# Second batch's fourth key block issued between W1's two transfers, its sums and key turns behind other work, in a Linformer attention and expert kernel on one core

## Chip, cores and metric

One core of a Trainium2 chip. The time is device microseconds of one execution; the figure for the kernel before is the median of three runs, 407.22 us (406.07 to 408.49).

## The reference, cut to what matters

Eight batches of eight heads of attention with 32 memory rows, then a mixture of experts in which each token goes to one expert.

```python
a = phi - np.max(phi, axis=2, keepdims=True); a = np.exp(a)
a = a / (np.sum(a, axis=2, keepdims=True) + 1e-09)
k_m = np.einsum('bhsm,bhsd->bhmd', a, k)
v_m = np.einsum('bhsm,bhsd->bhmd', a, v)
scores = scale * np.matmul(q, k_m.transpose(0, 1, 3, 2))
attn = softmax(scores)
x = attn @ v_m                      # [8 batches x 576 tokens, 512]
logits = normalised(x) @ normalised(expert_emb).T / tau
e = argmax(logits)                  # one expert a token
out = gate * (relu(x @ w1[e]) @ w2[e])
```

## The kernel before

The program is unrolled over batches. Each batch is treated as one group of tokens with one expert e, chosen from the batch's scores; tokens of another expert are counted and redone in a branch at the end. Because x is attn times v_m, the kernel multiplies v_m by W1 first (`project`, L655, two parts of 512 hidden columns, tiles `pg`, results `gh` and `gl`) and then attn by that product (`first`, L670, tiles `ph`), then by W2 (`second`, L692, tiles `py`). All engines run their instructions in the order in which the program writes them down. Eight banks of PSUM are handed out by rotation: `pt` takes t0, t1, ... over `tags` banks, `mm` takes m0 to m3; a tile waits until the bank's last reader is done.

The change lies in the opening, L985 to L1066, and in `batch(0)`, L821:

- Batch 0's scores are made, its first 128 tokens alone are weighed (`weigh`, `divide`, `turn`), and `choose` (L203) reads the expert from them. SP then loads that expert's W1 in two transfers of 1 MB (`load_w1`, L438), one for each part of `project`.
- Before that, `load_kv(1)` (L414, called at L1015) has put batch 1's keys and values into SP's queue: two pieces `kl` and four blocks `kx` of 512 KB, all ahead of W1.
- `fill` (L60) is a vector transpose of the scores of tokens 128 to 575 out of PSUM (tile `tr`), for both groups of heads, at L1045, behind the choice.
- `owner` (L220) is two small vector instructions on the counts; it stands ahead of the second `divide`.
- `slots(1, ...)` (L509) sums batch 1's keys and values over all blocks on TensorE into `acc0t` and `acc0m`. `scale(1)` (L534, two ScalarE instructions) and `again` (L556, one GpSimd copy) follow, all ahead of `project`.
- Between the two parts of `project(0)` the program has `part` (L637: two ScalarE casts and two GpSimd differences for `aT`), `keys(1)` (L543: two transposes `tk`, one ScalarE copy `kT`), `values(1)` (L560: two transposes `tv`, four copies `vT`; it reads both halves that `again` completes) and `attend(1, 2)` (L108: products `po` of two token tiles, their transposes `tt`, and the choice's `lg`, `m`, `oh` on VectorE). `norm(0)` (L175, one fused VectorE instruction that reads the bank m2, which the second part of `project` takes) stands ahead of the first part.
- `warm` issues matmuls whose result nobody reads.

Of the kernel before, what the change touches and what calls it, by code (L numbers as in the profile page):

```python
# [19 lines left out]
P = 128  # L20
B, H, S, D, M = 8, 8, 576, 64, 32
N, DM, E, FF = B * S, H * D, 8, 1024
NG = 2
# [23 lines left out]
class Tokens:  # L47
# [115 lines left out]
            out=self.oh[:, i], in0=self.lg[:, i], in1=self.m[:, i].unsqueeze(2).broadcast_to((P, len(ti), E)), op=ALU.is_equal  # L163
        )

    def turned(self, *ti):

        k, nc, b = self.k, self.nc, self.b
        t = self.pt([P, len(ti), NG * P], f"tt{b}_{ti[0]}")
        for n, i in enumerate(ti):  # L170
            for g in range(NG):
                nc.tensor.transpose(t[:, n, P * g : P * g + P], k.aw[:, g, T0[i] : T0[i] + P], k.ident)
        nc.scalar.copy(k.ea[:, ti[0] : ti[-1] + 1], t)
# [102 lines left out]
class Kernel:  # L276
# [137 lines left out]
    def load_kv(self, b):  # L414
        if b < B:
            for g in range(NG):
                to, x = self.kl[64 * g : 64 * g + 64], self.kvt[b, :, 4 * g : 4 * g + 4]
                (self.nc.sync if b else self.nc.scalar).dma_start(to, x)
            for k in range(4):
                self.nc.sync.dma_start(self.kx[k], self.kv[b, :, k])  # L420

    def load_q(self, b, halves=(0, 1)):
        if not b:
# [14 lines left out]
    def load_w1(self, e, halves=False):  # L438

        for k in range(2 if halves else 4):  # L440
            c, f = (slice(NC), slice(512 * k, 512 * k + 512)) if halves else (slice(k, k + 1), slice(FF))
            self.nc.sync.dma_start(self.w1s[:, c, f], self.w1[bass.ds(e, 1), :, c, f].rearrange("a p c f -> (a p) c f"))

# [377 lines left out]
    def batch(self, b, t, u):  # L821

        first, second = self.steps(b, t, u)
        self.halves = 0

        def must(f):
            while self.halves <= f:
                self.split_w()

        if b and u:  # L830
            self.keys(b + 1)
            self.values(b + 1)
        for k, _ in enumerate(self.project(b, self.vT[b % 2]) if u else ()):
            if not b:
                for g in range(NG):
                    self.part(g, slice(HS, S) if k else slice(P, HS), self.nc.scalar.copy)
                if k:
                    t.norm(1, 2)
                else:
                    self.keys(1)  # L840
                    self.values(1)
                    t.attend(1, 2)
        if b and u:

            self.scores(b + 1)
        for n, _ in enumerate(self.first(b)):
            for step in first[n]:
                step()
        for n, _ in enumerate(self.second(b, self.gate[:, b], self.rows(b), must)):
            for step in second[n]:  # L850
                step()
            if n == 8 and b == B - 1:
                left = self.others()
            if n == 24 and b == B - 1:
                self.tc.mark_branch_hint_location("others", left[1], engines=[ET.PE, ET.DVE, ET.SP, ET.Activation])
        return left if b == B - 1 else None
# [123 lines left out]
@with_exitstack  # L980
def moe_linformer(ctx, tc, phiT, qT, kv, kvt, emb, tau, w1, w2, out):
    k = Kernel(ctx, tc, phiT, qT, kv, kvt, emb, tau, w1, w2, out)
    ctx.enter_context(tc.manual_schedule(engines={ET.PE, ET.DVE, ET.Activation, ET.SP, ET.Pool}))


    k.eights()
    k.warm(11)
    k.load_phi(0)
    k.load_kv(0)
    k.load_q(0)  # L990
    k.load_router()
    k.consts()
    accs = [k.ps.tile([P, 2 * D], F32, tag=f"{n}3", name=f"acc0{n}", bufs=1) for n in "tm"]
    for vT in k.vT:
        k.nc.vector.memset(vT, 0.0)
    router = k.router()
    for g in range(NG):
        k.largest(0, g)
        k.softmax(0, (g,))
    for i in (0, 4, 8):  # L1000
        k.turn(0, i, min(i + 4, 9))
        if not i:
            next(router)
        if i < 8:
            k.warm(2 if i else 4)
    k.shares(0)
    next(router)
    k.load_phi(1)
    t = Tokens(k, 0, k.pt)
    for ks in ((0, 1), (4,), (2,), (3,)):  # L1010
        k.slots(0, accs, ks=ks, first=0 in ks, last=3 in ks)
        if ks[0] < 3:
            k.warm(2 if ks[0] == 2 else 1)
    k.scale(0)
    k.load_kv(1)  # L1015
    k.keys(0)
    k.again()
    first, others = slice(0, 4), slice(4, BL)
    ts = [k.mm([P, P], f"ts0_{g}", 1 + g) for g in range(NG)]
    k.score(0, ts, 0, P)  # L1020
    t.fill(range(NG), first, ts)
    next(router, None)
    k.values(0, copy=k.nc.scalar.copy)
    ts = [k.mm([P, S - P], f"tr0_{g}", g) for g in range(NG)]
    k.score(0, ts, P, S)
    k.squares(0, [k.pt([P, D + E], f"tl0_{g}") for g in range(NG)])
    list(t.weigh(range(NG), first))
    k.products(0)
    k.warm(5, 2)
    t.divide(range(NG), first)  # L1030
    t.turn(range(NG), first)
    k.largest(1, 0)
    k.softmax(1, (0,))
    t.attend(0, pt=lambda shape, name: k.mm(shape, name, 2), turned=False)
    e = t.choose((0,))
    t.turned(0)
    k.largest(1, 1)
    k.softmax(1, (1,))
    k.load_q(1, (0,))
    for i in (0, 4, 8):  # L1040
        k.turn(1, i, min(i + 4, 9))
        k.turns += not i
        if not i:
            k.warm(7, hot=t.spare)
    t.fill(range(NG), others, ts)  # L1045
    weights = [t.weigh((g,), others) for g in range(NG)]
    for g in range(NG):
        next(weights[g])
    for g in range(NG):
        next(weights[g])  # L1050
        list(weights[g])
    t.owner()
    k.shares(1, v=k.nc.gpsimd)
    for g in range(NG):
        k.part(g, slice(0, P), k.nc.scalar.copy)
    k.slots(1, accs)
    k.tags = 4
    k.scale(1)
    k.again(k.nc.gpsimd.tensor_copy)
    t.divide(range(NG), others, True)  # L1060
    t.turn(range(NG), others)
    t.norm(0)
    k.load_w2(e)
    k.load_q(1, (1,))
    k.load_phi(2)
    k.warm(3)  # L1066
    for b in range(B):
        u = Tokens(k, b + 1, k.pt) if b < B - 1 else None
        left = k.batch(b, t, u)
        t = u  # L1070
    k.rest(*left)
# [29 lines left out]
```

## Time and profile before

| what | value |
|---|---|
| median of three runs | 407.22 us |
| the profiled execution's own time | 406.74 us |
| its span, first to last instruction | 404.9 us |
| TensorE busy | 393.5 us, 97% of the span |
| VectorE, ScalarE, GpSimd busy | 65%, 39%, 42% |
| DMA, mean over the span | 225 GB/s |

The profile has a row for every instruction with its engine, line, tile and, where the engine stood idle before it, what released it. PE is TensorE's matmul row and PEld its weight loads; SPq is SP's queue, whose rows are the issue of a transfer and not its data.

### The profile page before, as it was taken

The numbers are of one execution on the slowest core, as the hardware profiler recorded it, in microseconds if no ns is written. First come the engines' busy times: TensorE is split into PE (matmuls) and PEld (weight loads), VectorE is DVE, ScalarE is ACT, GpSimd is POOL, SyncE is SP. The second block draws the span as 40 slices with busy tenths as digits, with TensorE's granted clock in tenths as the row PEclk, the third lists the DMA queues.
The fourth block names the chain that finished last, engine by engine and source line by source line (L and its number), as shares of the span: only waits on it lengthen the run. The fifth ranks groups of instructions, "written<-read, shape, count | busy, mean of one in ns | idle before, by whom it ended". The sixth has DMA issues, their size and how long they took to land. (4 is left out here: it accounts for less than half of the span.)

```text
span 404.9 us, 10350 instructions
## 1 busy us (share of the span) xinstructions
PE 393.5 (97%) x3933; PEld 318.5 (79%) x3933; DVE 262.3 (65%) x909; ACT 157.2 (39%) x430; POOL 171.2 (42%) x205
## 2 busy tenths in 40 slices
PE   7889999999999999999999999999999999999995
PEld 3458877798777978879787888879788897879784
DVE  4698795769664794758855795747936595745000
ACT  4366623165313633147311753137231561146110
POOL 1036563187133940369121961349303681329300
PEclk9999999999999999999999999999999999999999
DMA  8999927995679925995469926798359404790011
GB/s 265 345 363 357 375 61 183 342 358 212 149 255 386 349 46 132 346 384 234 74 215 389 387 82 160 251 388 338 56 137 361 178 2 81 249 396 6 14 53 56
DMA packets 69862, 91.24 MB, mean 225 GB/s; under 512 B 41800, under 2 KB 47688, under 8 KB 69808
## 3 DMA queue, kind: packets, MB, share of 16 engines
q1 hardware_dynamic: 66928, 82.00, 60.9%
q0 software_dynamic: 2688, 8.26, 5.8%
q8 instruction: 32, 0.52, 0.5%
q10 hardware_dynamic: 192, 0.28, 0.2%
q14 instruction: 22, 0.18, 0.1%
HBM read 71.19 MB, written 19.33 MB: 224 GB/s over the span
## 5 line engine op out<-in xcount | busy, mean ns | idle before, releaser
L681 PE MATMUL ph<-aT,gh 128*128 128x288 f32 x512 | 103.2, 297 | 0.0
L734 PE MATMUL py<-wh,hh 128*128 128x512 f32 x248 | 99.3, 400 | 0.0
L734 PE MATMUL py<-wh,hl 128*128 128x512 f32 x248 | 96.7, 390 | 0.0
L734 PE MATMUL py<-wl,hh 128*128 128x512 f32 x248 | 96.7, 390 | 0.0
L652 POOL TENSOR_TENSOR wl<-w2s,wh 128x512 fp32r<-128x512 f32 x64 | 85.1, 1330 | 5.0
L681 PEld LDWEIGHTS ph<-aT,gh 128*128 128x128 f32 x512 | 81.8, 188 | 1.7 <-DVE oh L162 0.8
L681 PE MATMUL ph<-aT,gl 128*128 128x288 f32 x256 | 75.4, 294 | 0.0
L687 DVE SCALAR_TENSOR_TENSOR hl<-ph,hh 128x288 fp32r<-128x288 f32 x128 | 55.8, 450 | 22.1 <-ACT hh L684 16.7
L739 ACT ACTIVATE ys<-py,gate 128x512 f32<-128x512 f32 (+1 forms) x39 | 25.1, 642 | 105.3 <-PE py L734 70.3
L684 ACT ACTIVATE hh<-ph 128x288 fp32r<-128x288 f32 x128 | 52.4, 417 | 31.9 <-PE ph L681 31.6
L868 POOL DMA_DIRECT2D out_dram<-ys x28 | 15.5, 553 | 106.1 <-ACT ys L739 69.4
L734 PEld LDWEIGHTS py<-wh,hh 128*128 128x128 f32 x248 | 46.5, 188 | 14.6 <-issue 4.9
L734 PEld LDWEIGHTS py<-wh,hl 128*128 128x128 f32 x248 | 46.6, 188 | 10.1
L734 PEld LDWEIGHTS py<-wl,hh 128*128 128x128 f32 x248 | 46.6, 188 | 9.0
L681 PEld LDWEIGHTS ph<-aT,gl 128*128 128x128 f32 x256 | 48.0, 188 | 0.0
L642 POOL TENSOR_TENSOR aT<-aw,aT 128x576 fp32r<-128x576 f32 (+3 forms) x20 | 23.7, 1204 | 48.4 <-DVE aT L641 42.8
L651 POOL CAST wh<-w2s 128x512 fp32r<-128x512 f32 x62 | 38.6, 622 | 1.0 <-DMA w2s<-w 0.9
L723 PE MATMUL py<-w2s,h 128*64 128x256 f32 x256 | 29.4, 382 | 0.0
L665 DVE TENSOR_TENSOR gl<-pg,gh 128x512 fp32r<-128x512 f32 x32 | 20.0, 684 | 8.7 <-ACT gh L664 8.7
L723 PEld LDWEIGHTS py<-w2s,h 128*64 128x64 f32 x256 | 17.7, 137 | 9.3 <-DVE hl L687 1.0
L472 ACT ACTIVATE ex<-ex,nm 128x576 f32<-128x576 f32 x16 | 12.3, 771 | 29.5 <-DVE nm L457 29.5
L664 ACT CAST gh<-pg 128x512 fp32r<-128x512 f32 x32 | 16.5, 599 | 10.5 <-PE pg L662 10.5
(180 smaller groups left out, 468.9 us busy)
## 6 DMA issues: line engine op xcount, KB each, us to landing
kx<-kv SPq DMA_DIRECT2D x32, 512.0 KB, 7.5
w2s<-w SPq DMA_DIRECT2D x32, 512.0 KB, 9.8
w1s<-w SPq DMA_DIRECT2D x28, 512.0 KB, 6.4
out_dram<-ys POOLq DMA_DIRECT2D x28, 256.0 KB, 6.1
qt<-qT SPq DMA_DIRECT2D x12, 576.0 KB, 8.8
ad<-aw SPq DMA_DIRECT2D x8, 576.0 KB, 12.5
td<-x SPq DMA_DIRECT2D x56, 72.0 KB, 2.1
ea<-td SPq DMA_DIRECT2D x7, 512.0 KB, 4.4
```

The costliest lines, as they stand in the source:

```text
L642: self.nc.gpsimd.tensor_tensor(out=al, in0=a, in1=ah.bitcast(F32), op=ALU.subtract)
L651: (copy or self.nc.scalar.copy)(h, x)
L652: self.nc.gpsimd.tensor_tensor(out=l, in0=x, in1=h.bitcast(F32), op=ALU.subtract)
L664: nc.scalar.copy(self.gh[:, g, f], ps[g])
L665: nc.vector.tensor_tensor(out=self.gl[:, g, f], in0=ps[g], in1=self.gh[:, g, f].bitcast(F32), op=ALU.subtract)
L681: nc.tensor.matmul(p, lhsT=w[:, g, fs], rhs=x[:, g, to], start=g == 0 and k == 0, stop=g == 1 and k == 2)
L684: nc.scalar.activation(self.hh[:, f, to], p, AF.Relu)
L687: nc.vector.scalar_tensor_tensor(out=self.hl[:, f, to], in0=p, scalar=0.0, in1=self.hh[:, f, to].bitcast(F32), op0=ALU.max, op1=ALU.subtract)
L723: nc.tensor.matmul(p[64 * j : 64 * j + 64], lhsT=self.h4[:, f], rhs=self.w2s[:, f, d * j : d * j + d], start=f == 0, stop=f == 7,)
L734: nc.tensor.matmul(p, lhsT=h[:, f, to], rhs=w[:, f], start=f == 0 and k == 0, stop=f == 7 and k == 2)
L739: nc.scalar.activation(y[:, :d], p, AF.Copy, scale=gate[:, i : i + 1])
L868: eng.dma_start(self.out[r : r + P], y)
```

## The change

Batch 1's fourth block `kx[3]` is issued between W1's two transfers. Its sum stands behind the first part of `project(0)`, and so do `scale(1)`, `again` and `norm(0)`. `keys(1)` and `values(1)` go behind `attend(1, 2)`, and the transposes `tt` of those two token tiles take the bank m0 instead of a t bank. The vector transposes of the scores are split: group 0's goes ahead of the first 128 tokens' `divide`, group 1's stays. `owner` goes behind the second `turn`.

```diff
-    def turned(self, *ti):
+    def turned(self, *ti, pt=None):
-        t = self.pt([P, len(ti), NG * P], f"tt{b}_{ti[0]}")
+        t = (pt or self.pt)([P, len(ti), NG * P], f"tt{b}_{ti[0]}")
...
-            for k in range(4):
-                self.nc.sync.dma_start(self.kx[k], self.kv[b, :, k])
+            for k in range(3 if b == 1 else 4):
+                self.load_block(b, k)
+
+    def load_block(self, b, k):
+        self.nc.sync.dma_start(self.kx[k], self.kv[b, :, k])
...
         for k in range(2 if halves else 4):
+            if halves and k:
+                self.load_block(1, 3)
...
                 else:
+                    self.slots(1, ks=(3,), first=False)
+                    self.tags = 4
+                    self.scale(1)
+                    self.again(self.nc.gpsimd.tensor_copy)
+                    t.norm(0)
+                    t.attend(1, 2, turned=False)
+                    t.turned(1, 2, pt=lambda shape, name: self.mm(shape, name, 0))
                     self.keys(1)
                     self.values(1)
-                    t.attend(1, 2)
...
     list(t.weigh(range(NG), first))
+    t.fill((0,), others, ts)
     k.products(0)
...
-    t.fill(range(NG), others, ts)
+    t.fill((1,), others, ts)
...
-    t.owner()
     k.shares(1, v=k.nc.gpsimd)
     for g in range(NG):
         k.part(g, slice(0, P), k.nc.scalar.copy)
-    k.slots(1, accs)
-    k.tags = 4
-    k.scale(1)
-    k.again(k.nc.gpsimd.tensor_copy)
+    k.slots(1, accs, ks=(0, 1, 4, 2), last=False)
     t.divide(range(NG), others, True)
     t.turn(range(NG), others)
-    t.norm(0)
+    t.owner()
```

## Rows read from the trace of the kernel before

**Rows 1.** Busy time of each engine in two stretches: stretch, its length, engines, clock, DMA, GB/s.
```profile
32.00:62.00 30.00, 30.00 (x250) 25.57 (x239) 26.07 (x76) 14.32 (x43) 17.72 (x20) 1.00 0.76 259
62.00:404.00 342.00, 337.17 (x3372) 279.17 (x3370) 213.95 (x760) 126.89 (x343) 147.71 (x165) 1.00 0.65 214
```

**Rows 2.** TensorE in order of time, 22 to 32.6 us: start, us, instruction, count, idle before.
```profile
25.03 0.42 PE L522 MATMUL acc0t<-kx,eT 128*32 128x128 f32 x8 [0.85 <-DMA kx<-kv]
...
26.64 0.82 PE L396 MATMUL hot<-ones 128*128 128x512 bf16 x3
27.80 1.09 PE L662 MATMUL pg<-w1s,vT 64*32 64x512 f32 x16 [0.34 <-DMA w1s<-w]
28.83 0.44 PE L547 MATMUL tk<-ident,ks 128*128 128x128 f32 x2
...
29.32 1.09 PE L119 MATMUL po<-vv,aw 128*128 128x136 f32 x8
30.77 0.66 PE L172 MATMUL tt<-ident,aw 128*128 128x128 f32 x4 [0.36 <-ACT kT L551]
31.36 1.09 PE L662 MATMUL pg<-w1s,vT 64*32 64x512 f32 x16
```

**Rows 3.** SP's issues in order of time, and W1's transfers with their median time to landing.
```profile
15.98 0.43 SPq L420 DMA_DIRECT2D kx<-kv  x1
...
21.67 1.37 SPq L442 DMA_DIRECT2D w1s<-w  x2
...
w1s<-w SPq DMA_DIRECT2D x2, 1024.0 KB, 6.0
```

**Rows 4.** All engines in short stretches, for their last columns (DMA share, GB/s).
```profile
22.50:22.75 0.25, 0.25 (x5) 0.23 (x3) 0.25 (x1) 0.22 (x1) 0.15 (x2) 1.00 0.24 98
...
23.25:23.50 0.25, 0.25 (x16) 0.23 (x9) 0.25 (x2) 0.25 (x1) 0.19 (x2) 1.00 0.47 139
...
24.00:26.00 2.00, 1.15 (x44) 0.97 (x40) 1.93 (x6) 1.48 (x4) 1.34 (x4) 1.00 1.04 392
```

**Rows 5.** VectorE in order of time.
```profile
16.93 0.42 DVE L83 TENSOR_REDUCE z<-x 128x8 f32<-128x256 f32 x1 [0.82 <-ACT x L75]
...
21.23 1.16 DVE L64 STREAM_TRANSPOSE x<-tr 128x448 f32<-128x448 f32 x2
...
24.86 0.17 DVE L487 RECIPROCAL rs<-rs 128x2 f32<-128x2 f32 x1
...
29.07 0.20 DVE L94 STREAM_TRANSPOSE aw<-x 128x64 f32<-128x64 f32 x1
29.20 0.39 DVE L182 CUSTOM_DVE_ANT_0 ea<-po,ea 128x256 f32<-128x256 f32 x1
...
29.54 1.29 DVE L665 TENSOR_TENSOR gl<-pg,gh 128x512 fp32r<-128x512 f32 x2
```

**Rows 6.** ScalarE and GpSimd in order of time.
```profile
22.64 2.17 POOL L483 TENSOR_SCALAR rs<-sm 128x1 f32<-128x1 f32 x5
...
27.07 0.36 ACT L539 ACTIVATE ks<-acc0m,rs 128x128 f32<-128x128 f32 x1
27.49 0.48 POOL L558 COPY ks<-ks 128x128 f32<-128x128 f32 x1 [1.20 <-ACT ks L539]
...
28.93 1.07 ACT L664 CAST gh<-pg 128x512 fp32r<-128x512 f32 x2 [1.50 <-PE pg L662]
29.89 0.56 ACT L641 CAST aT<-aw 128x160 fp32r<-128x160 f32 x2
30.30 1.00 POOL L642 TENSOR_TENSOR aT<-aw,aT 128x160 fp32r<-128x160 f32 x2 [2.33 <-ACT aT L641]
```

**Rows 7.** TensorE early in the run: the scores, and two groups of warming matmuls.
```profile
1.02 4.13 PE L396 MATMUL hot<-ones 128*128 128x512 bf16 x11 [1.02 <-DVE ones L334]
...
16.42 0.58 PE L582 MATMUL tr<-qt,kT 64*32 64x448 f32 x4
...
17.06 1.25 PE L396 MATMUL hot<-ones 128*128 128x512 bf16 x5
```

## The prediction

> **What bounds the kernel now.** I read the busy time of each engine over the whole run first, and asked in which stretch TensorE is not full. From 32 us to 62 us it is busy for 30.00 of 30.00 us, and from there to 404 us for 337.17 of 342.00 [rows 1]. So from 32 us on the kernel is a row of matmuls, and a delay or a gain of TensorE at 32 us comes out at the end almost whole. Everything that the change touches lies ahead of that. What counts is one number: when the second part of `project(0)` starts, 31.36 us now, since batch 0's `ph` matmuls follow it without a gap [rows 2].
>
> Then I read TensorE in order of time to that point. It waits for `kx[3]` until 25.03 us, finishes the sums, warms itself, waits 0.34 us for W1's first half and starts the first part at 27.80. Then come `tk`, `tv`, `po`, a wait of 0.36 us for `kT`, `tt`, and the second part at 31.36 [rows 2]. The waits that can be saved add up to 0.34 + 0.36 = 0.7 us between 27 and 31 us. All the rest there is matmuls, or has another reason: `po` starts at 29.32 because VectorE's last transpose of `aw` ends at 29.27 [rows 2, 5].
>
> Last I read SP's issues and the DMA rate beside them. `kx[3]` is issued at 15.98, W1's two halves from 21.67 [rows 3]. Between 22.5 and 23.5 us the 16 DMA engines move only 98 to 139 GB/s, and 392 GB/s once W1 is flowing [rows 4]. This is the row on which the forecast turns: `kx[3]` has left the queue before W1's data begin, so the queue runs dry waiting for the choice of the expert. W1's first half doesn't stand behind `kx[3]`; it stands behind its own issue.
>
> **Taking `kx[3]` out from ahead of W1.** W1's first half lands 6.0 us after its issue, at 27.67 [rows 3]. With the queue dry before it, taking 0.5 MB away only makes the dry stretch longer. Gain: 0, with 0.5 us at most if the tail of `kx[3]`, at a DMA share of 0.24 [rows 4], holds W1's first packets. I take 0 because a queue at a quarter of its rate is not what holds a transfer.
>
> The Trainium skill (DMA: Bandwidth & Descriptors, Latency and other measured facts) gives about 0.6 us from the issue of such a transfer to its first byte. By that W1 could flow from 22.3 us, while the trace still shows `kx[3]` draining, and the change would gain some 0.3 us here; the low rate up to 23.5 us speaks against it.
>
> **Putting it behind W1's first half.** The block's data now follow 1 MB of W1. At 392 GB/s 524 KB take 1.33 us [rows 4], so it lands at 27.67 + 1.33 = 29.0 us instead of 25.03 [rows 2, 3]. The bounds are 28.5 (W1 0.5 us earlier) and 29.6 us: `kx[3]` was seen by TensorE some 2.2 us after the rate had collapsed at 22.75, W1's half, by 392 GB/s, some 1.6 us after its last byte, and the block may have the longer of the two. W1's second half lands 1.33 us later as well; at 392 GB/s two halves and the block take 6.69 us, from some 23.25 us (where 1.6 us before 27.67 less 2.68 us of data lies) to 30.0, and with 1.6 us behind that it lands at 31.6.
>
> The Trainium skill (the same page, Anatomy of one DMA) puts most of a transfer's fixed 2 us into the receipt of its last byte. The trace agrees, with 1.6 to 2.2 us; with 2.0 the block would land 0.4 us later.
>
> **The split `fill`.** One of two transposes, 1.16 / 2 = 0.58 us [rows 5], moves ahead of the reduction at 16.93 us that leads to the choice. VectorE has 0.82 us of idle time there, waiting for ScalarE. But the transpose needs group 0's scores, whose matmuls are the first eight of sixteen; the last four run from 16.42 to 17.00 [rows 7], so group 0 is done at about 16.5. The transpose ends at 17.1 instead of 16.93: the choice, W1's issue and all behind it come 0.17 us later. Bounds: 0 (group 0 done by 16.3) and 0.65 (done only at 17.0). What it frees at 21.23 is worth nothing: VectorE's next stage passes through the reciprocal at 24.86, which waits for GpSimd's five instructions from 22.64 to 24.81 [rows 5, 6]. `owner`, two instructions of the size of that reciprocal, some 0.4 us, leaves the place ahead of it for the same nothing, and takes `norm(0)`'s place ahead of `gl`.
>
> **TensorE's new order.** Behind the first part (27.80 + 0.17 to 29.06) TensorE is now held for `kx[3]` until 29.0 + 0.17 = 29.17. Its sums are two groups' shares of one block; one took 0.42 [rows 2] and the two overlap, 0.65 us: 29.82. Then `po` 1.09 and, as spaced now, 0.59 for `tt`: 31.50. The wait for `kT` is gone, since `tt` has its own bank; m0 is free when VectorE's first `gl` is done, near 30.5. `tk` and `tv` take 29.32 - 28.83 = 0.49 [rows 2]. They used to run while VectorE finished `aw`, at no cost; now they stand at the end: 31.99. By TensorE alone the second part starts 0.63 us later than now.
>
> **Three queues behind the block.** `scale`, `again` and `norm(0)` are moved past other work. ScalarE: the two `gh` casts and two `aT` casts end at 30.45 + 0.17 = 30.62 [rows 6], then `scale`'s two. Each is 0.36 and they overlap, 0.63: 31.25; `tk` is in time. GpSimd: the differences for `aT` end at 31.30 + 0.17 = 31.47, and only then comes `again`, 0.48 [rows 6]: 31.95. `tv` reads what `again` writes, so it starts at 32.0 and not at 31.77; with 0.25 for `tv` the second part starts at 32.25. VectorE: `aw` ends at 29.44, `owner` 29.84, `gl` 1.29, then `norm(0)`, 0.39 [rows 5]: 31.55. The second part needs `norm(0)` because it takes bank m2, and it is in time. The bank rotation of t0 to t3 shifts by one for everything after; `attend(3, 4)` then needs `norm(1)` one tile earlier, with about 0.1 us to spare, and I cost that at nothing (0.3 if the cover is gone).
>
> **The sum.** 32.25 - 31.36 = +0.9 us: 0.17 from the early transpose, 0.46 from the block's landing and from `tk` and `tv`, which lost their cover (less the 0.36 us wait that goes), and 0.26 from `again`. On the profiled execution, 406.74 us with a span of 404.9, this gives 407.6; it stands 0.48 us under the median 407.22, so I add the 0.9 us to the median: 408.1 us.
>
> **Rivals.**
> *W1's first half does come earlier, by 0.5 us.* For it: the DMA share is not zero while `kx[3]` ends [rows 4], and TensorE does wait for W1 [rows 2]. Then the block lands at 28.5 and `po` is held by `aw` at 29.3 to 29.5 again. TensorE's row from there is 1.09 + 0.59 + 0.49 = 2.17 us, so the second part starts at 31.5 to 31.7: +0.3 us, 407.5. Nothing here gets under 31.36, because VectorE's `aw` sets the start.
> *A net gain.* `aw` itself comes earlier: if the freed 1.0 us of VectorE lets GpSimd's five instructions through sooner (they take 2.17 us, 0.43 each, where VectorE's reciprocal of like size takes 0.17 [rows 5, 6]), the reciprocal and the whole chain move by up to 0.5 us, and W1 earlier adds to it. 31.46 - 0.5 is 0.4 us before now: 406.8. Against it: VectorE's subtraction still runs beside GpSimd there.
> *Slower: TensorE's clock.* The sums now end near 25.0 and the three warming matmuls near 25.9; up to W1's landing at 27.8 TensorE would stand idle for 1.9 us, more than any gap now, then again until 29.17. The granted clock is 1.00, the 2.4 GHz level, in every stretch that I read [rows 1, 4]. A fall to 1.2 GHz would cost what the slow opening shows: eleven warming matmuls took 4.13 us, five later ones 1.25 [rows 7], so eleven cost 4.13 - 2.75 = 1.4 us more. With the 0.9 us: +2.3, 409.5. It passes the bound from 1.1 us of such loss on.
> *The change doesn't do what it says* is my forecast itself: the order of issue changes, the landing of W1 does not.
>
> **How the numbers follow.** Forecast (+0.9) 0.55, W1 earlier (+0.3) 0.25, net gain (-0.4) 0.08, clock (+2.3) 0.12. Summing the bounds on the forecast gives +0.2 to +2.1 us. The three runs before spread by 1.2 us to either side, which is as large as the effect. So the range goes from 406.3 (the net gain with some of that spread) to 409.9 us (the clock case with some of it). About 0.5%, 2 us, can be told from no change. Faster by that needs more than all the waits named, 0.04. Slower by it is most of the clock case and the upper end of the forecast, 0.13. Within it 0.83.
>
> **What would show it.** In the changed kernel's profile: W1 issued at 21.7 to 21.9 and the first `pg` at 27.7 to 28.1 (right) or at 27.3 and earlier (the first rival); a longer dry stretch of the DMA ahead of W1; the sums of `kx[3]` starting near 29.2 with a wait for DMA; `tv` just behind GpSimd's `again` near 32; the second part of `pg` at 32.25; the clock at 1.00 from 25 to 33 us. The forecast is wrong if the second part starts ahead of 31.4, or if TensorE's full row from 32 us on has gaps that take the delay up.

## The result, and the profile after

| | before | after |
|---|---|---|
| median, us | 406.8 (22 executions, 405.42 to 408.49) | 409.02 (22 executions, 407.2 to 411.59) |
| ratio to before | | 1.0057 [1.0044, 1.007] |
| profiled execution: time, span, us | 406.74, 404.9 | 411.02, 409.2 |
| second part of `pg` starts, us | 31.36 [rows 2] | 34.69 |

The change costs 2.3 us. The forecast was +0.9 (408.1); the time is inside its range, but the loss is two and a half times the forecast, and it lies just past the 0.5% that can be told from no change, where the forecast had put 0.13. The forecast of the time looks better than that of the loss because it stood on the 407.22 of three runs, 0.4 us above the median of 22.

The profiled execution of the changed kernel is one of the longer ones. Its loss is there before TensorE's full row begins. This is TensorE of the changed kernel in order of time (start, us, instruction, count, idle before), which answers to [rows 2]:

```profile
26.70 1.09 PE L667 MATMUL pg<-w1s,vT 64*32 64x512 f32 x16 [1.23 <-DMA w1s<-w]
29.86 0.66 PE L527 MATMUL acc0t<-kx,eT 128*32 128x128 f32 x8 [2.07 <-DMA kx<-kv]
30.29 0.65 PE L527 MATMUL acc0m<-kx,eT 128*32 128x128 f32 x8
30.87 2.18 PE L119 MATMUL po<-vv,aw 128*128 128x136 f32 x8
32.85 1.06 PE L172 MATMUL tt<-ident,aw 128*128 128x128 f32 x4
33.70 0.63 PE L552 MATMUL tk<-ident,ks 128*128 128x128 f32 x2
34.13 0.64 PE L569 MATMUL tv<-ident,ks 128*128 128x128 f32 x2
34.69 1.78 PE L667 MATMUL pg<-w1s,vT 64*32 64x512 f32 x16
```

The wait of 0.34 us for W1 has become 1.23, the 0.36 for `kT` is gone, and a wait of 2.07 for the block is new. From 29.86 on each group takes 1.6 to 2 times as long as before: `po` 2.18 instead of 1.09, `tt` 1.06 instead of 0.66, `pg` 1.78 instead of 1.09. The second part ends at 36.47 instead of 32.45, 4.0 us later, and the span is 4.3 us longer.

SP's issues (start, us, instruction) answer to [rows 3]:

```profile
21.39 0.63 SPq L447 DMA_DIRECT2D w1s<-w  x1
22.12 0.56 SPq L423 DMA_DIRECT2D kx<-kv  x1
22.90 0.58 SPq L447 DMA_DIRECT2D w1s<-w  x1
```

The block now stands between the halves. TensorE starts on W1's first half 26.70 - 21.39 = 5.31 us after its issue (6.13 before), on the block 29.86 - 22.12 = 7.74 us after its own.

The trace also tells when W1's second half landed, in this kernel and in the one before, where nothing shows a wait for it. It holds the start and length of every packet and counts the completion of each transfer in sixteen steps; the sixteenth is the landing, and wherever TensorE waits for a transfer in these profiles it starts 0.04 to 0.14 us behind that. W1's second half landed at 30.76 us before and at 32.50 after: 9.09 and 11.11 us after W1's first issue. So before, the second part began 0.60 us behind the landing, and in this execution of the changed kernel 2.19 us behind it.

All engines in some stretches (stretch, its length, busy time and count of PE, PEld, DVE, ACT, POOL, granted clock, DMA share, GB/s) answer to [rows 4]:

```profile
22.25:22.50 0.25, 0.25 (x4) 0.19 (x2) 0.25 (x1) 0.19 (x1) 0.16 (x2) 1.00 0.00 0
22.50:22.75 0.25, 0.25 (x3) 0.14 (x1) 0.25 (x2) 0.00 (x0) 0.17 (x2) 1.00 0.00 0
22.75:23.00 0.25, 0.25 (x9) 0.18 (x12) 0.25 (x1) 0.23 (x1) 0.25 (x1) 1.00 1.00 172
...
24.00:26.00 2.00, 1.47 (x33) 0.46 (x23) 1.38 (x4) 0.85 (x4) 1.28 (x4) 1.00 1.01 367
26.00:28.00 2.00, 1.09 (x16) 0.21 (x16) 1.91 (x3) 0.18 (x1) 0.00 (x0) 1.00 0.87 256
28.00:29.25 1.25, 0.00 (x0) 0.00 (x0) 1.22 (x7) 1.25 (x4) 0.05 (x1) 1.00 1.00 380
29.25:36.00 6.75, 6.14 (x48) 4.31 (x48) 2.66 (x10) 2.09 (x7) 1.24 (x3) 0.51 1.04 413
```

Three things are to be seen. The queue is empty until 22.75, where before a remnant of `kx[3]` moved at 98 to 139 GB/s. From 26 to 28 us, where the block's data must pass, the rate is 256 GB/s and not 367 to 392; 256 times 2.0 us is just the block's 0.5 MB. And from 29.25 to 36 us the granted clock is 0.51, the 1.2 GHz level, behind the 2.07 us in which TensorE stood idle.

### The profile page after: what moved, and what is told of

It is laid out like the page before. It is cut to its first block, busy times and chain, and to the rows that moved or that the text cites. A ratio compares the mean times of both kernels' runs of the same rounds, so it can differ in the third digit from the quotient of the medians.

```text
span 409.2 us, 10351 instructions
## 1 busy us (share of the span) xinstructions
PE 396.9 (97%) x3933; PEld 320.4 (78%) x3933; DVE 262.0 (64%) x909; ACT 157.3 (38%) x430; POOL 170.9 (42%) x205
```

## The experiments

The theories. **Landing:** the block's 0.5 MB pushes W1's second half, and with it the second part, back. **Order:** `tk`, `tv` and `again` at the end cost it, as the prediction has it. **Clock:** the idle stretches lower TensorE's clock. "Issue to part 2" below is the time from W1's first issue to the start of the second part of `pg`, which takes out the opening's own scatter: W1 is issued between 20.98 and 22.42 us in the profiles of this study. Edits are against the changed kernel unless the text says otherwise.

**1. The changed kernel once more.** No edit.

> The changed kernel once more, beside the others on the same chip. Two theories. Theory idle: TensorE's long idle stretches (1.2 us ahead of the first part of project, 2.07 us ahead of the sums of the fourth block, in the changed kernel's profile) let its clock fall to 0.50 in some executions, and each fall costs some 2.7 us on top of a fixed 1.2 us; then the runs split, those with a mean granted clock of 0.996 and more near 408 us and those of 0.994 and less near 410.5 us. Theory order: the loss is the new order of work, 1 to 2 us in every run, and the clock is a matter of the chip; then the runs don't split by clock, and the kernel before shows the low clock as often. Median expected 408.5 to 409.5 us.

Measured: 409.67 us, 1.0064 [1.004, 1.0088]. With the 22 executions above these are 28. In 11 the mean granted clock was 0.990 to 0.994; their median is 410.5 us. In the other 17 it was 0.996 or more: 408.25. So the clock falls at least in four executions of ten, and those are 2.25 us longer; but the others are still some 1.45 us slower than before. The loss has two parts, and the clock is the smaller one: 11/28 of 2.25 is 0.9 us on the mean. A mean of 0.996 does not exclude a short fall (10); one of the 17 has just that.

This profile is also one with a fall (0.994; 0.50 from 32 to 34 us). W1's second half landed at 33.04, and the second part began at 34.57.

**2. TensorE kept busy in the idle stretches.**

```
     k.load_phi(2)
-    k.warm(3)
+    k.warm(8)
...
+                    self.warm(8, hot=t.spare)
                     self.slots(1, ks=(3,), first=False)
```

> The changed kernel with matmuls that nobody reads put into both idle stretches: eight ahead of the first part of project instead of three, and eight between that part and the sums of the fourth block. Nothing else moves. Theory idle: the clock stays at 1.00 throughout, every run shows 0.996 or more, the slow group is gone, the median falls to 407.6 to 408.3 us, some 1.2 us above the kernel before. Theory order: same as the changed kernel, 408.5 to 409.5 us, with or without a fall of the clock.

Measured: 409.56 us, 1.008 [1.0047, 1.0114], with no mean clock under 0.996 in seven executions. The edit overshot: the eight matmuls ahead of the sums run from 29.37 to 31.24, past the block's landing, and in the profiled execution W1's first half came 6.99 us after its issue. That it is slow proves nothing, though it is just above what theory order had; that the clock is held and nothing is won is a first sign against the clock as the main cause.

**3. The block early, everything else as changed.**

```
-            for k in range(3 if b == 1 else 4):
+            for k in range(4):
                 self.load_block(b, k)
...
-            if halves and k:
-                self.load_block(1, 3)
```

> The changed kernel with all four blocks issued ahead of W1 again, as before; the sums of the fourth block and everything behind them stay where the change put them. Theory idle, with the block's late landing as the cause: the block has landed long before its sums, the 2.07 us wait goes, the sums follow the first part of project at once, the clock stays up; what is left is the transposes of the keys and values behind the token tiles and the copy behind GpSimd's differences, so the second part of project starts 0.3 to 0.8 us later than before: 407.1 to 407.7 us. Theory order: the loss stays whole, 408.5 us and more.

Measured: 407.56 us, 1.0025 [1.0003, 1.0046], with a clock under 0.996 in two of twelve. More than half of the loss goes with the block's place in the queue. TensorE of this kernel, same columns as above:

```profile
28.95 1.74 PE L119 MATMUL po<-vv,aw 128*128 128x136 f32 x8
30.56 0.66 PE L172 MATMUL tt<-ident,aw 128*128 128x128 f32 x4
...
31.59 1.09 PE L665 MATMUL pg<-w1s,vT 64*32 64x512 f32 x16
```

With the sums, `tk` and `tv` still late, the second part is back at 31.59, 9.54 us from W1's issue (before: 31.36 - 21.67 = 9.69). `po` takes 1.74 us because its second token tile waits for a bank that `owner`, now late, still reads.

**4. Only the issue moved.** Against the kernel before, only the `load_block` parts of the change; the sums stay ahead of the first part of `pg`.

> The kernel before with the order of issue alone changed: the fourth block between W1's two transfers, all work as it was, so that its sums stand ahead of the first part of project. TensorE then waits for the block ahead of everything. If the block again lands some 7.7 us after its issue, near 29.8 us, TensorE starts the first part 2.5 to 3 us later than before, and stands idle for 4 us and more ahead of it: with a fall of the clock 411 to 414 us, without one 409 to 410 us. If the block follows W1's half by 1.33 us, as the prediction had it, it lands near 28.5 us, and the time is 408.0 to 408.8 us without a fall. It also shows whether the block's data flow at 250 GB/s again, as in the changed kernel's profile from 26 to 28 us, or at 390.

Measured: 412.8 us, 1.0148 [1.0122, 1.0173].

```profile
30.79 0.66 PE L527 MATMUL acc0t<-kx,eT 128*32 128x128 f32 x8 [6.09 <-DMA kx<-kv]
```

TensorE starts on the block 30.79 - 23.14 = 7.65 us after its issue, as in the changed kernel, and everything stands behind it; behind that wait the clock is under 0.996 in five of the six executions. So the rest of the change, above all the sums behind the first part, earns back some 3.7 us of the 6 that the move of the issue costs.

**5. A smaller filling.** As 2, with `self.warm(4, hot=t.spare)` and `k.warm(6)`.

> The changed kernel with fewer matmuls that nobody reads than in the run with eight and eight: six ahead of the first part of project, four behind it. Their 0.9 us (four at 0.22) fit into the 2.07 us wait for the block with 1 us to spare, where eight ran past the block's landing. Theory idle: the clock stays at 0.996 and more in every run and the matmuls delay nothing, so the time is that of the changed kernel's runs without a fall, 407.9 to 408.6 us. If holding the clock is worth nothing in itself, the time stays at 409 to 409.7 us with the clock up.

Measured: 409.09 us, 1.005 [1.0031, 1.007]; clock under 0.996 in two of twelve.

```profile
29.49 1.01 PE L396 MATMUL key<-ones 128*128 128x504 bf16 x4 [1.50 <-DVE own L225]
...
33.05 1.09 PE L667 MATMUL pg<-w1s,vT 64*32 64x512 f32 x16
```

The warming matmuls waited themselves, 1.50 us, for `owner` to let go of their bank. With the clock at 1.00 throughout this profile the second part still starts at 33.05, 11.47 us from W1's issue. That is 0.13 us behind the landing of W1's second half (32.92), though no wait stands at that row.

**6. Keys first.**

```
                     t.norm(0)
+                    self.keys(1)
+                    self.values(1)
                     t.attend(1, 2, turned=False)
                     t.turned(1, 2, pt=lambda shape, name: self.mm(shape, name, 0))
-                    self.keys(1)
-                    self.values(1)
```

> The changed kernel with the turns of keys and values ahead of the two token tiles again, still behind the fourth block's sums. The prediction priced their place at the end at 0.5 us with the copy on GpSimd behind the differences. If that term is right, TensorE now waits there for the copy instead, so that the second part of project starts 0.2 to 0.6 us later or earlier only by as much, and the median stays within 0.6 us of the changed kernel's, 408.6 to 409.8 us. If the block's landing alone sets the time, it is the same: 409 to 409.7 us, with the same falls of the clock in about four runs of ten.

Measured: 409.4 us, 1.0059 [1.0039, 1.008]: as the change. In this profile the block came 28.81 - 22.25 = 6.56 us after its issue, with a wait of 0.88 us only,

```profile
28.81 0.50 PE L527 MATMUL acc0t<-kx,eT 128*32 128x128 f32 x8 [0.88 <-DMA kx<-kv]
```

and the second part was no earlier for it: 33.24, 11.71 us from W1's issue. W1's second half had landed at 32.85, so it could have started 0.3 us earlier at most; what kept it was TensorE's own row at a granted clock of 0.50 from 30 to 32 us. Seven of the twelve executions have a clock under 0.996, and here they are no longer than the other five (medians 409.32 and 409.48): a fall that is over by the time W1 lands would cost nothing, which fits but is not shown. Neither the order of keys and token tiles nor an earlier landing of the block moves the end.

**7. All but the block.** Against the kernel before: `tt` in bank m0, the split `fill`, `owner` behind the second turn; the block is loaded and summed as before.

> All of the change but the fourth block's move: the block is issued and summed where it was, with scale, the copy and norm(0) where they were; the split vector transposes, owner behind the second turn, and the token tiles' transposes in bank m0 stay. Theory: the block's move is the whole loss, and the rest is worth the 0.36 us wait for kT at most, less 0.15 us for the early transpose: 406.0 to 406.6 us, not to be told from the kernel before. If the rest of the order costs, 407 us and more.

Measured: 407.73 us, 1.0008 [0.9986, 1.0029]; the expectation had 406.0 to 406.6, and 407 and more if the rest costs. By the ratios the change less this one is 0.0049, 2.0 us, for the block's move together with the late sums and the order behind them. By the medians of the runs side by side this kernel is 0.95 us slower than before (407.73 and 406.78), so that more of the loss would be the rest; a difference of 0.002 is not to be read closer than that. TensorE, then VectorE of this kernel:

```profile
28.10 0.44 PE L550 MATMUL tk<-ident,ks 128*128 128x128 f32 x2
30.15 0.66 PE L567 MATMUL tv<-ident,ks 128*128 128x128 f32 x2 [1.62 <-POOL aT L645]
...
29.78 0.23 DVE L225 TENSOR_SCALAR own<-key,cm 128x8 f32<-128x8 f32 x1
```

The profile names GpSimd's `aT` as the releaser of `tv`, but `tv` takes the bank that `owner` reads, and `owner` ends at 30.01, 0.14 us ahead of it. Behind that wait the granted clock is 0.50 from 31 to 33 us, and the second part starts at 33.33, 2.59 us behind the landing of W1's second half: a late start without any transfer between the halves.

**8. `tt` in bank m0 and nothing else,** against the kernel before:

```
-                    t.attend(1, 2)
+                    t.attend(1, 2, turned=False)
+                    t.turned(1, 2, pt=lambda shape, name: self.mm(shape, name, 0))
```

> The kernel before with one part of the change alone: the two token tiles' transposes take bank m0. The 0.36 us wait for the copy kT goes, and nothing else is late in its place before 30.5 us: 406.0 to 406.3 us, 0.1 to 0.4 us under the kernel before, which may be too little to tell.

Measured: 406.6 us, 0.9974 [0.9955, 0.9993], the lowest ratio of the study. It is faster than the change; against before the interval ends just below 1 and the medians are 0.2 us apart (406.78), so a gain is likely but hardly told.

```profile
29.63 0.66 PE L172 MATMUL tt<-ident,aw 128*128 128x128 f32 x4
...
31.02 1.09 PE L662 MATMUL pg<-w1s,vT 64*32 64x512 f32 x16 [0.73 <-DMA w1s<-w]
```

The wait of 0.36 us for `kT` [rows 2] is gone from `tt`, and now the second part waits 0.73 us for W1's second half: TensorE starts on it 31.02 - 21.06 = 9.96 us after W1's issue, the latest of the six kernels with nothing between the halves. In the kernel before it had landed 9.09 us after the issue and TensorE came at 9.69; the slack was 0.60 us.

**9. The gaps filled without a wait.** As 5, with six matmuls in each gap and those ahead of the sums in bank t2:

```
+                    self.warm(6, hot=self.ps.tile([P, 512], F32, tag="t2", name="hotg", bufs=1))
                     self.slots(1, ks=(3,), first=False)
...
-    k.warm(3)
+    k.warm(6)
```

> The changed kernel with six matmuls that nobody reads ahead of the first part of project and six between it and the sums of the fourth block, now in bank t2, which is free. In the two runs before this, those behind the first part were in the bank that holds the counts for owner, and in one profile they waited 1.50 us for it and ended behind the block's landing. Theory idle: with the gap really filled from 28 us on, the clock is 0.996 and more in every run, and the time is that of the changed kernel's undisturbed executions, 407.9 to 408.6 us: what is left above the kernel before, 1.2 to 1.8 us, is the block's landing. Rival: the clock is held and the time stays at 409 us and more, so the falls are not what costs.

Measured: 409.13 us, 1.0046 [1.0023, 1.0069], and no mean clock under 0.996 in twelve executions. SP, then TensorE:

```profile
22.21 0.62 SPq L447 DMA_DIRECT2D w1s<-w  x1
...
30.05 0.43 PE L527 MATMUL acc0t<-kx,eT 128*32 128x128 f32 x8
32.31 0.38 PE L569 MATMUL tv<-ident,ks 128*128 128x128 f32 x2
33.73 1.09 PE L667 MATMUL pg<-w1s,vT 64*32 64x512 f32 x16 [1.03 <-DMA w1s<-w]
```

This profile has everything of the change and the clock at 1.00, TensorE is done with the block, `tk` and `tv` at 32.7, and it waits 1.03 us for W1's second half: 11.52 us after W1's issue. On the clock of before (issue at 21.67) that is 33.19, 1.83 us later than 31.36; the measured ratio is worth 1.9 us.

**10. Early block, `owner` in its old place.** As 3, and `t.owner()` again ahead of `k.shares(1, ...)`.

> The changed kernel with the block issued ahead of W1 as before, and owner back ahead of the second divide. In the run with the early block alone the second token tile's product waited for owner, which holds bank t1 until 29.8 us, while TensorE stood idle for about 0.6 us. If that wait is what was left there, the time is the kernel before's within its spread, 406.2 to 407.0 us, with no clock under 0.996; if the order of keys, values and the copy behind the token tiles costs by itself, 407.2 to 407.8 us as without this edit.

Measured: 407.38 us, 1.0014 [0.9994, 1.0035]. Against 3 no difference can be told, as the expectation had it if the order costs by itself. In this profile a fall follows the wait for W1's first half alone:

```profile
27.04 1.93 PE L665 MATMUL pg<-w1s,vT 64*32 64x512 f32 x16 [1.88 <-DMA w1s<-w]
```

The granted clock is 0.50 from 28 to 30 us, and the second part starts 11.23 us after W1's issue, 2.34 behind the landing of its second half. The mean over the execution is still 0.996: by that figure alone up to three of the 19 executions of 2 and 9 may hold such a fall.

**11. As 7, `owner` in its old place:** `tt` in m0 and the split `fill` alone.

> All of the change but the block's move and owner's move: the split vector transposes and the token tiles' transposes in bank m0. In the run that also had owner behind the turn, the values' turns waited 1.62 us for bank t1, which owner still read, and the clock fell to 0.50. With owner back that wait goes: 405.9 to 406.7 us, 0 to 0.9 us under the kernel before and the fastest of all; if the early transpose costs more than the 0.15 us seen in the changed kernel's profile, 406.8 us and more.

Measured: 406.45 us, 0.9988 [0.997, 1.0005]. Experiment 10 has this and the late sums with the order behind them; it is 0.93 us slower in medians (beside the same runs of before; the intervals overlap).

**12. Nothing but the bytes.** Against the kernel before, a transfer of the same 0.5 MB between W1's halves, into a place that nothing reads any more; the block itself is loaded and summed as before.

```
         for k in range(2 if halves else 4):
+            if halves and k:
+                self.nc.sync.dma_start(self.qt[:, :2, :512], self.kv[1, :, 3].rearrange("p (a h) d -> p a (h d)", a=2))
```

> The kernel before, all work and its order as it was, with one more transfer of 512 KB that nobody reads (the fourth block once more, into space for batch 0's queries, which are done) issued between W1's two halves. It prices what the change's transfer does to W1's second half and nothing else. Theory second half: in the profile of the token tiles in m0 the second part of project already waited 0.73 us for W1's second half, which landed 9.96 us after the first half's issue; in the changed kernel with filled gaps it waited 1.03 us and started 11.5 us after that issue. So the second part has no slack, the extra transfer delays it by 1.3 to 2.0 us less some 0.3 us of slack, with a wait for DMA on w1s in the profile: 1.0 to 1.7 us above the kernel before, 407.8 to 408.6 us, clock up. Rival, that the fourth block's own landing, or the falls of the clock, is the whole loss: then this costs nothing, 406.4 to 407.2 us.

Measured: 408.96 us, 1.0054 [1.0035, 1.0073]. That is the whole loss of the change (1.0057), with none of its other parts. Clock 0.993 to 0.995 in seven of twelve; those have a median of 409.42, the other five 408.85, so the loss is there with the clock held, as in this profile (1.00). SP's issues, TensorE, VectorE, two microseconds of all engines, and W1's two transfers (shortest, median and longest time from the issue of each to its landing):

```profile
22.37 0.62 SPq L444 DMA_DIRECT2D w1s<-w  x1
23.09 0.56 SPq L442 DMA_DIRECT2D qt<-kv  x1
23.86 0.58 SPq L444 DMA_DIRECT2D w1s<-w  x1
...
29.31 1.09 PE L664 MATMUL pg<-w1s,vT 64*32 64x512 f32 x16 [1.77 <-DMA w1s<-w]
...
33.83 1.09 PE L664 MATMUL pg<-w1s,vT 64*32 64x512 f32 x16 [0.90 <-DVE oh L162]
...
33.55 0.18 DVE L162 TENSOR_TENSOR oh<-lg,m 128x16 bf16<-128x16 f32 x1
...
27.00:29.00 2.00, 0.54 (x3) 0.04 (x1) 1.90 (x4) 0.50 (x2) 1.09 (x1) 1.00 0.85 252
...
DMA to landing us min/median/max: 6.8/8.3/9.8
```

The second part starts 33.83 - 22.37 = 11.46 us after W1's issue, as in 5, 6 and 9. The profile puts its wait of 0.90 us to VectorE's `oh`. It was W1: the second half landed 9.8 us after its own issue at 23.86, at 33.70, 0.13 ahead of the start, and in the kernel before `oh` ran after the second part had started. The 0.5 MB again pass at 252 GB/s, 2.0 us.

Set side by side, in us from W1's first issue; the landing is that of W1's second half, the clock that of the profile up to the second part:

| kernel | 0.5 MB between the halves | landing | part 2 starts | clock | ratio |
|---|---|---|---|---|---|
| before | no | 9.09 | 9.69 | held | 1 |
| `tt` in m0 (8) | no | 9.91 | 9.96 | held | 0.9974 |
| `tt` in m0, split `fill` (11) | no | 8.81 | 9.13 | held | 0.9988 |
| early block (3) | no | 9.13 | 9.54 | held | 1.0025 |
| early block, `owner` back (10) | no | 8.89 | 11.23 | fell | 1.0014 |
| all but the block (7) | no | 8.95 | 11.54 | fell | 1.0008 |
| the change | yes | 11.11 | 13.30 | fell | 1.0057 |
| the change again (1) | yes | 11.39 | 12.92 | fell | 1.0064 |
| gaps filled too far (2) | yes | 11.28 | 12.39 | held | 1.008 |
| only the issue moved (4) | yes | 11.03 | 16.36 | fell | 1.0148 |
| gaps filled, some (5) | yes | 11.34 | 11.47 | held | 1.005 |
| keys first (6) | yes | 11.32 | 11.71 | fell | 1.0059 |
| gaps filled (9) | yes | 11.38 | 11.52 | held | 1.0046 |
| bytes alone (12) | yes | 11.33 | 11.46 | held | 1.0054 |

The landing falls into two groups that do not touch: 8.81 to 9.91 us without the transfer between the halves, 11.03 to 11.39 with it. The second part never starts ahead of it. In 5, 8, 9 and 12 it starts right behind it; in the others something else is later still, and where the clock fell it is TensorE's own row, with or without the transfer.

## Why the prediction was right or wrong

**That the start of the second part decides: right, roughly.** Its delay comes back in the time, as in 9: 1.83 us seen, 1.9 measured. Profile by profile it is looser: the times of the thirteen other profiles differ from before's by their delay and -0.4 to +1.6 us more.

**The covered transfer: the step that failed.** The prediction let W1's second half land at 31.6, ahead of a second part at 32.25, and left it at that. From W1's issue at 21.67 this is 9.93 us with the block in between, and 8.6 without the block's 1.33. The profiles of the change show 11.11 and 11.39, which is 32.8 to 33.1 on before's clock, behind 32.25 and not ahead of it. About 0.5 of the miss was there already in the kernel before (9.09), and the rest is the block: it moves the landing by some 2.3 us (from about 9.0 to 11.3), where the prediction had 1.33. What the sum left out is the last of the sixteen counts. In the two profiles of the change fifteen are in at 9.84 and 9.94, as forecast; the sixteenth comes 1.27 and 1.46 later, with packets that end as much later. Before, it came 0.43 behind the fifteenth. In every profile one packet of 16 KB of instructions takes about 1 us somewhere from 26.7 to 29.2 us, and in six of the eight kernels with the transfer between the halves the long lag first shows in the transfer that is moving then or the next one; that the packet causes it is not shown.

The row that the estimate started from, 6.0 us from issue to landing [rows 3], is W1's first half alone, and the prediction took "no wait" for slack. The slack was 0.60 us in the kernel before, 0.32 in 11 and 0.04 in 8. That this could become the bound should have been a rival: it gives a second part at 32.9 to 33.2, +1.5 to +1.8 us. That the measured time is inside the range all the same is owed to the range's width, which was made for the clock and the spread of the runs, and not to this path.

**392 GB/s for the block: too high, and made up for.** The block passed at 252 and 256 GB/s, in 2.0 us instead of 1.33. But from the last byte to TensorE the prediction allowed 1.6 to 2.2 us, and read the trace as agreeing with a fixed 2 us; it does not. The last packet of W1's second half ends 0.43 to 0.46 us ahead of the landing in all fourteen profiles. The two errors work against each other, so that the forecast fits fifteen counts of sixteen is in part luck. (One of its sums is off by 0.14 as well: 27.67 less 1.6 and 2.68 is 23.39, not 23.25.)

**W1's first half does not come earlier: right, and more firmly than it was argued.** The dry stretch ahead of W1 grew, to a rate of 0 until 22.75, as forecast. W1's first packet starts 1.41 to 1.45 us after its issue in all fourteen profiles, whether the queue is dry by then (the change) or still moves `kx[3]` (before, 12): taking the block out from ahead gains nothing. From issue to TensorE the half took 5.31 us in the profile after, against 6.13 before, but that is scatter: it took 5.28 to 5.34 (3, 7, 8) as well as 6.06 (10, 11) with nothing behind it but its other half, and 6.94 with the unread transfer behind it (12). Fifteen of its sixteen counts are in 4.97 to 5.40 us after the issue in every profile; the sixteenth makes the difference. The Trainium skill (DMA: Bandwidth & Descriptors, Latency and other measured facts) gives about 0.6 us from issue to first byte; the trace shows 1.41 to 1.45. By the page's figure, as an estimate, W1 would have flowed 0.8 us sooner.

**The block behind the first half.** Forecast 29.0 to 29.2, bounds 28.5 to 29.6; seen 29.86 in the profile after (7.74 us from its issue), 28.81 in 6 (6.56), 30.79 in 4 (7.65). The place is right. The scatter, which was not in the bounds, is again the sixteenth count: in the profile after fifteen were in at 28.58 and the last at 29.82.

**The split `fill`: right.** VectorE, ScalarE and VectorE again, of the changed kernel:

```profile
16.13 0.65 DVE L64 STREAM_TRANSPOSE x<-tr 128x448 f32<-128x448 f32 x1 [0.36 <-PE tr L587]
16.70 0.38 DVE L83 TENSOR_REDUCE z<-x 128x8 f32<-128x256 f32 x1
...
16.14 0.42 ACT L75 ACTIVATE x<-x 128x256 f32<-128x256 f32 x1
...
24.57 0.17 DVE L492 RECIPROCAL rs<-rs 128x2 f32<-128x2 f32 x1 [0.90 <-POOL rs L488]
```

ScalarE is done at 16.56 and the reduction starts at 16.70: 0.14 us behind it, 0.03 before; forecast +0.17, seen +0.11. What is freed later ends in a wait of 0.90 us for GpSimd ahead of the reciprocal, as the prediction said. W1's issue is even 0.28 us earlier than before, within the opening's scatter.

**The order of `tk`, `tv` and `again`: hidden, not refuted; `again` itself wrong.** The sum had 0.72 us for the order together with the block's landing. In the full change W1's second half comes after all of it, so turning the order round changes nothing (6). With the block early and `owner` back (10 against 11) the late sums and their order are 0.93 us slower, though the two intervals overlap and falls of the clock may be in it. The 0.26 for `again` did not come true: GpSimd ended it well ahead of `tv` at 34.13,

```profile
31.53 0.29 POOL L563 COPY ks<-ks 128x128 f32<-128x128 f32 x1 [1.33 <-ACT ks L544]
```

at 31.82, and in 9, with the clock held, at 31.58 ahead of `tv` at 32.31.

**`owner` for nothing: a step missed.** It was priced by VectorE's time, and its price is the bank that it reads. In 7 `tv` stood 1.62 us for it, and in 5 the warming matmuls did, 1.50. In the change itself TensorE is waiting for the block by then, so no cost shows there. By time alone 7 (1.0008) and 11 (0.9988) lie 0.002 apart, with intervals that overlap.

**The clock rival: it happens, as a part.** It was given 0.12 and an extra 1.4 us. It shows in 11 of 28 executions, with 2.25 us between them and the rest. Its place was right: in the wait for the block or behind it. The two profiles of the change show how it costs: the second part began 2.19 and 1.53 us behind W1's landing, so there TensorE's row at half its clock came last, and not W1. But it is not what makes the median slow: filled gaps, with no mean under 0.996 in 19 executions (2 and 9), left 1.008 and 1.0046, and 12 loses as much with the clock held. Filling the gaps won nothing that can be told (1.0046 and 1.005 against 1.0057).

**In sum.** On the landing of W1's second half the change gives some +1.3 us (issue at 21.39) to +1.8 (issue at before's 21.67); the 17 executions with a mean of 0.996 and more show +1.45, and the falls add about 0.9 on the mean: 2.2 to 2.7, measured 2.3. No profile of the unedited change with the clock held was taken, so that its second part would start on W1's landing there is inferred from 5, 9 and 12. The block's own landing is a bound of nearly the same height in the change: with the 2.64 us from the sums to the end of `tv` in 9, the second part could start at 32.50 and 33.19 in its two profiles by the block, at 32.63 and 33.17 by W1. That W1's half is enough by itself is shown by 12, which has no such path and the whole loss; and in 5 and 9, where the block landed earlier, the second part still started on W1's landing.

## What to carry to other kernels

Before a transfer is put ahead of another, find when that other one lands, not whether anybody waits for it: no wait can mean next to no slack, and an edit that makes its reader earlier (here `tt` in another bank) uses up what there is. A landing is that of the transfer's last part, and a sum of bytes over a mean rate gives that of most of it. The bytes moved within a shared queue are paid by every later transfer in it, so price them at each reader that is just in time, and test them by themselves with a transfer that nobody reads. An instruction moved for nothing on its own engine can still hold a PSUM bank that another engine needs.

## What the runs showed of the hardware

- 1 MB of W1 took 5.28 to 6.99 us from issue to its reader from one execution to another. Fifteen of its sixteen completion counts were in after 4.97 to 5.40 us; the last came up to 1.87 us later, and why is open.
- W1's first packet started 1.41 to 1.45 us after the issue in all fourteen profiles, into an empty queue or not; the last packet of its second half ended 0.43 to 0.46 us ahead of the landing.
- 0.5 MB queued between two transfers of 1 MB passed at 252 and 256 GB/s, at a DMA share of 0.85 and 0.87, where 367 to 392 GB/s flow around it. The source alone does not make it so: other blocks of the same `kv` pass at 408 GB/s from 19 to 22 us in the kernel before. What does is open.
- Behind waits for a DMA of 1.23 and 2.07 us the granted clock was 0.51 for 6.75 us in one execution of the change; behind a wait of 1.88 us in 10 it was 0.50 from 28 to 30 us. Other executions of the same kernels kept a mean of 0.996 and more.
